# Five instruction lists written out as a table, in place of a planner, for a linear-attention and snake-MLP kernel

## The chip, the cores and the metric

The kernel runs on one core of one Trainium2 chip. The metric is the device time of one execution in microseconds; lower is better. The engines are PE (TensorE matmul, with PEld its weight loads), ACT (ScalarE), DVE (VectorE), POOL (GpSimd) and SP (SyncE, which here only issues DMAs).

## The reference

Two stages. First a blocked linear attention with decay over q, k, v of shape (4, 8, 768, 64):

```python
intra = np.einsum('bhic,bhjc->bhij', qb, kb) * Dmask[None]
intra = np.einsum('bhij,bhjd->bhid', intra, vb)
inter = np.einsum('bhid,bhde->bhie', qb * lam_pow[None], kv_state)
out[:, :, sl] = intra + inter
kv_state = lam_block * kv_state + np.einsum('bhsd,bhse->bhde', kb_dec, vb)
```

Its output, as x of 3072 tokens by 512, goes through an MLP with a snake activation, d_ff = 2048:

```python
h = x @ w_in
s = np.sin(alpha * h)
g = h + s * s / (alpha + 1e-09)
return g @ w_out
```

Inputs and output are float32; the kernel multiplies in bf16.

## The kernel before, in words

The attention works on 24 blocks of 128 tokens, six for each of 4 batches. For each block q and k are scaled by decay factors (`scale_block`, on POOL and DVE) and v is cast (ACT); q and k are transposed, on PE for the first blocks and by a DMA transpose on SP from block 12 on (`piece_T`, L565); then PE makes the masked scores, the block's output and the state (`piece_G`), DVE masks the scores (Sm, L687), and ACT or DVE copies the state (Zd, Zc) and the output (xT) out of PSUM. Loads are issued by SP (L379), those of the later weights by POOL.

The MLP works on 6 chunks of 512 tokens. `unit_A` and `unit_A2` make one tile of h: PE multiplies into a PSUM bank (L886, L920), ACT takes the sine (t16), ACT or POOL squares it (u16), and DVE adds h and writes gT (`scalar_tensor_tensor`, L903 and L938); that last step frees the bank. In the later chunks these products rotate over banks 4, 5 and 6. The second product is `unit_B` (L951) for chunks 0 and 1. For chunks 2 to 5 it is a scheme with seven products i of half size (`unit_P`, L1039) in place of eight, on sums of weights (`weight_sums`, L994) and sums of tokens (`token_sums`, L1017, on POOL or DVE); `finish` and `finish_half` (L1085, L1061, DVE) combine the products into osb rows and issue the stores (SP, some on ACT, L1089, L1094, L1063; stores of chunks 0 and 1 by ACT at L971).

All work is recorded first, as 1040 operations by `op(...)`, numbered from 0 in the order of the calls, each with what it reads and writes, so that dependences are known. Some operations name several engines that may run them. Then `_settle` decides the engine of each and the order on every engine, and `emit` writes the instructions in this order; where an operation depends on another engine, it waits on a semaphore. On every engine the instructions run in the order written. Before the change `_settle` is a planner on the host: it walks through modelled time, gives each engine its next ready operation by preference, and `MOVES` shifts the preferences of groups of operations. Dependences alone make the result right, so any order that keeps them computes the same.

Numbers used below: 99 cast of the second quarter of w1; 124, 130 the `unit_A2` of chunk 0 for its tokens 0 to 255 and 256 to 511; 136, 140, 163 `unit_A` of chunk 0; 138 a square and 139 an L903 step of chunk 0; 198, 200 casts of v, 215 and 218 a block's k transposed and copied, 221 a `piece_G`, 238 a copy to osb; 239, 240, 243, 244, 247, 248, 324, 325 stores of chunk 0; 290 a copy to xT; 204, 205, 339, 415, 422, 547 loads of k or v; 559, 595 to 597, 788 token sums; 594, 609, 613 L903 steps; 599 a `unit_B` of chunk 1; 604 a sum of weights; 635 a `unit_A` of chunk 3 into bank 4; 770 a cast of v. In the last chunk: 1031, 1034, 1037 the products i = 7 (the second token half in two parts), 1032, 1035, 1038 the subtractions after them and 1033, 1036, 1039 their stores; 1014, 1017, 1020 the stores of i = 5; 1027, 1030 those of the rows of i = 2 and 6.

Of the kernel before, what the change touches and what calls it, by code (L numbers as in the profile page):

```python
# [33 lines left out]
class _Plan:  # L34

    AHEAD = 40
    WINDOW = {"PE": 0.3, "ACT": 0.1, "DVE": 0.1, "POOL": 0.1}
    PIPE = {"ACT": 0.11, "DVE": 0.09, "POOL": 0.045, "PE": 0.0}
    HOP = {"PE": 0.055, "ACT": 0.035, "DVE": 0.035, "POOL": 0.075, "SP": 0.1}
    DRAIN = 0.085  # L40
    MOVES = (
        (633, 30, "any", 60), (169, 3, "all", 60), (138, 30, "all", -100), (112, 1, "SP", -10),
        (104, 1, "all", 210), (421, 3, "SP", -5), (967, 30, "PE", 145), (272, 3, "all", -155),
        (442, 3, "all", 60), (352, 30, "all", -145), (807, 3, "all", -15), (534, 10, "all", -15),
        (957, 30, "all", -25), (281, 30, "all", -55), (232, 30, "all", 40), (680, 1, "PE", 40),
        (1000, 3, "all", 55), (486, 1, "DVE", 55),
    )
    SPIN = ((0.095, 112, 5.0), (0.056, 128, 9.4), (0.216, 512, 1e9))
# [32 lines left out]
    @staticmethod  # L81
    def _transfers(order):

        queues = {}
        for o in order:
            if o.dma is not None:
                queues.setdefault(o.eng, []).append(o)
        left = {e: [[o.start + o.lag, o.runs, o.dur / o.runs, o] for o in sorted(q, key=lambda o: o.start)]
                for e, q in queues.items()}
        now, lands = 0.0, {}  # L90
        while any(left.values()):
            heads = [q[0] for q in left.values() if q]
            on = [h for h in heads if h[0] <= now]
            later = [h[0] for h in heads if h[0] > now]
            if not on:
                now = min(later)
                continue
            turn = sum(h[2] for h in on)
            step = min([h[1] * turn for h in on] + [t - now for t in later])
            now += step  # L100
            for h in on:
                h[1] -= step / turn
                if h[1] < 1e-6:
                    lands[h[3]] = now + h[3].lat
                    left[h[3].eng].pop(0)
        return lands

    def _settle(self):

        prio = {o: i - o.lead for i, o in enumerate(self.ops)}  # L110
        for at, width, kind, by in self.MOVES:
            for o in self.ops[at:at + width]:
                if (kind == "all" and o.given != "SP") or o.given == kind or (kind == "any" and not isinstance(o.given, str)):
                    prio[o] += by
        lands, best = {}, None
        for _ in range(10):
            order, new, off = self._pass(prio, lands)
            if best is None or off < best[0]:
                best = off, order, [(o, o.eng, o.start, o.done) for o in order]
            if off < 0.5:  # L120
                break
            lands = new
        for o, eng, start, done in best[2]:
            o.eng, o.start, o.done = eng, start, done
        return best[1]

    def _pass(self, prio, lands):
        for o in self.ops:
            o.eng, o.start, o.done = o.given, None, None
        order = self._order(prio, lands)  # L130
        new = self._transfers(order)
        return order, new, sum(abs(t - o.done) for o, t in new.items())

    def _order(self, prio, lands):
        num = {o: i for i, o in enumerate(self.ops)}
        waits = {o: len(o.deps) for o in self.ops}
        after = {}
        for o in self.ops:
            for d in o.deps:
                after.setdefault(d, []).append(o)  # L140
        clock = {e: 0.8 for e in ("PE", "SP", "ACT", "DVE", "POOL")}
        wire, port = 0.0, 0.0
        filler = self.filler
        sp = sorted((o for o in self.ops if o.eng == "SP"), key=lambda o: (prio[o], num[o]))
        pe = [o for o in self.ops if o.eng == "PE"]
        place = {o: i for i, o in enumerate(pe)}
        left = len(self.ops)
        can = {o for o in self.ops if not waits[o]}
        at = {}

        def ready(o, e):
            t = clock[e]
            for d in o.deps:
                if d.eng == e and (e == "PE" or d.dma is not None):
                    t = max(t, d.done)
                else:
                    t = max(t, d.done + self.HOP[e] + (self.DRAIN if d.eng == "PE" else 0.0))
            return t

        order = []  # L160
        nsp, npe = 0, 0
        while left:
            while npe < len(pe) and pe[npe].start is not None:
                npe += 1
            per = {e: [] for e in clock}
            for o in can:
                if o.eng == "SP":
                    if o is sp[nsp]:
                        per["SP"].append((at.setdefault(o, ready(o, "SP")), 0, o, o.dur))
                    continue  # L170
                if isinstance(o.eng, str):
                    e, d = o.eng, o.dur
                    if e == "PE" and place[o] >= npe + self.AHEAD:
                        continue
                    t = ready(o, e)
                else:
                    _, e, t, d = min((ready(o, e) + d + late, e, ready(o, e), d) for e, d, late in o.eng)
                if o.port:
                    t = max(t, port)
                per[e].append((t, prio[o], o, d))  # L180
            best = None
            for e, c in per.items():
                if not c:
                    continue
                soon = min(x[0] for x in c) + self.WINDOW.get(e, 0.0)
                x = min((x for x in c if x[0] <= soon), key=lambda x: (x[1], num[x[2]]))
                if best is None or x[0] < best[0]:
                    best = x[0], x[2], e, x[3]
            t, o, e, dur = best
            if e == "SP":  # L190
                t = max(t, clock["SP"])
                nsp += 1
            if e == "PE" and filler is not None:
                emit, reads, last = filler
                if last.start is not None:
                    filler = None
                else:
                    deps = [self.writer[b] for b in reads]
                    free = max([clock["PE"]] + [d.done + self.HOP["PE"] if d.done is not None else t for d in deps])
                    one, cols = next((d, n) for d, n, end in self.SPIN if free < end)  # L200
                    n = int((t - free) / one)
                    if n > 0:
                        f = _Op("PE", lambda h, n=n, cols=cols: emit(h, n, cols), one * n, tuple(reads), (), None, (), 0, 0)
                        f.deps = set(deps)
                        f.start, f.done = free, free + one * n
                        order.append(f)
            o.eng, o.start = e, t
            if o.dma is not None:
                clock[e] = t + o.issue
                wire = max(wire, t + o.lag) + o.dur  # L210
                o.done = max(t + o.lag + o.dur + o.lat, lands[o]) if o in lands else wire + o.lat
            else:
                o.done = t + dur
                clock[e] = o.done - self.PIPE[e]
                if o.port and e != "ACT":
                    port = o.done
            order.append(o)
            can.discard(o)
            left -= 1
            for s in after.get(o, ()):  # L220
                waits[s] -= 1
                if not waits[s]:
                    can.add(s)
        return order
# [48 lines left out]
def bass_lightning_attn__then__act_snake_kernel(  # L273
# [38 lines left out]
    with es:  # L312
# [15 lines left out]
        t16 = ring("t16", RU, [128, TCH], BF16)  # L328
        u16 = ring("u16", RU, [128, TCH], BF16)
# [8 lines left out]
        v32 = sb("v32", [128, RL * H * D], F32)  # L338
        qk2 = sb("qk2", [128, R2, 2 * H, D], BF16)
        v2 = sb("v2", [128, R2, H, D], BF16)  # L340
# [27 lines left out]
        def _(_unused_eng):  # L368
# [4 lines left out]
            op = P.op  # L373
# [84 lines left out]
            last = {}  # L458
# [22 lines left out]
            for i in range(3):  # L481
                t, ks = (4, 2) if i < 2 else (2, 1)
# [31 lines left out]
            def ported(o):  # L514
                o.port = True
                return o
# [793 lines left out]
```

## Time and profile before

| what | us |
|---|---|
| median of 3 runs (lowest to highest) | 213.34 (212.63 to 217.04) |
| profiled execution, its own time | 213.08 |
| its span in the profile | 211.3 |
| PE busy | 202.5 |
| ACT, DVE, POOL busy | 162.7, 151.2, 148.5 |
| mean granted PE clock | 0.999 |

Span is the time from the first to the last instruction of the program; the execution's own time has 1.8 us more around it. A row of a group gives the count after x, then busy time and mean duration in ns; a row of a wait gives who waited, for whom, the sum in us, how often, and the longest. In a table of stretches each engine's busy us is followed by its number of instructions, then the granted PE clock, the share of the DMA engines and GB/s. In a timeline a row has start, duration, engine, line, operation and tiles.

### The profile page before, as it was taken

To read this page: it belongs to the slowest core of one execution; us is meant where nothing else is said; L and a number is where in the kernel's file an instruction comes from. 1 tells how busy PE (TensorE), PEld (TensorE's weight loads), DVE (VectorE), ACT (ScalarE), POOL (GpSimd) and SP (SyncE) were. 2 spreads that over 40 slices of the span, in tenths; PEclk is the share of its full clock that TensorE was granted. 3 is DMA by queue.
4 is the path that set the end of the run, shared out by engine and by line. 5 is a ranking of instruction groups with operands and counts; after the bars stand their busy time and mean duration, and the time that the engine had idled before them with its cause. 6 is when DMAs were issued, how large, how long until landed. Compare 5 with 4: busy or idle time off the path is not lost.

```text
span 211.3 us, 4847 instructions
## 1 busy us (share of the span) xinstructions
PE 202.5 (96%) x1947; PEld 134.7 (64%) x1975; DVE 151.2 (72%) x237; ACT 162.7 (77%) x306; POOL 148.5 (70%) x147
## 2 busy tenths in 40 slices
PE   7988999999999999999999999999999999999995
PEld 7955534446677775645447677666667656666994
DVE  4884567684879896699989697565777657847553
ACT  4859895745988998798977998989698789767001
POOL 7085369583597668388998979879973678976660
PEclk9999999999999999999999999999999999999999
DMA  4999999999999999999969591335000050000514
GB/s 144 309 318 228 206 212 228 230 213 288 244 243 263 241 208 253 182 246 220 232 141 259 91 174 27 64 133 105 5 0 3 2 199 0 3 0 0 200 52 149
DMA packets 78998, 33.35 MB, mean 158 GB/s; under 512 B 55408, under 2 KB 76160, under 8 KB 78976
## 3 DMA queue, kind: packets, MB, share of 16 engines
q1 hardware_dynamic: 73744, 27.14, 56.6%
q0 software_dynamic: 3696, 3.67, 10.6%
q10 hardware_dynamic: 1536, 2.24, 3.3%
q8 instruction: 15, 0.25, 0.5%
q14 instruction: 7, 0.06, 0.1%
HBM read 27.28 MB, written 6.29 MB: 159 GB/s over the span
## 4 chain that ended last, share of the span: by engine, by line
PE 65%; ACT 13%; DVE 11%; DMA 3%; SPq 3%; issue 2%; ACTq 1%; POOL 0%
PE bank L1039 21%; PE bank L886 20%; PE bank L951 9%; PE bank L920 6%; DVE gT L903 5%; DMA v<-in_v_dram 3%; SPq L379 3%; PE bank L780 2%; PE bank L676 2%; ACT t L930 2%; ACT u L900 2%; ACT t L896 2%; ACT Zd L730 2%; DVE Xs L1017 1%; ACT v L559 1%
## 5 line engine op out<-in xcount | busy, mean ns | idle before, releaser
L903 DVE SCALAR_TENSOR_TENSOR gT<-u,rinv,bank 128x512 bf16<-128x512 bf16 x74 | 54.0, 743 | 26.7 <-ACT u L900 26.5
L886 PE MATMUL bank<-xT,w 128*128 128x512 bf16 x277 | 68.3, 379 | 2.3 <-DVE w L448 0.5
L896 ACT ACTIVATE t<-bank,alpha 128x512 bf16<-128x512 f32 x74 | 49.4, 683 | 14.0 <-PE bank L886 12.8
L1017 POOL TENSOR_TENSOR gT<-gT 128x512 bf16<-128x512 bf16 x37 | 43.1, 1175 | 8.1 <-DVE gT L903 3.7
L886 PEld LDWEIGHTS bank<-xT,w 128*128 128x128 bf16 x296 | 28.2, 98 | 29.5 <-DVE gT L903 2.3
L900 ACT ACTIVATE u<-t 128x512 bf16<-128x512 bf16 x66 | 41.0, 630 | 2.4 <-DVE gT L903 0.9
L1017 POOL TENSOR_TENSOR Xs<-gT 128x512 bf16<-128x512 bf16 x23 | 27.3, 1185 | 10.5 <-DVE gT L903 10.1
L687 DVE TENSOR_TENSOR Sm<-bank,mask 128x1024 bf16<-128x1024 f32 x24 | 29.0, 1220 | 4.0 <-PE bank L676 1.6
L951 PE MATMUL bank<-w,gT 128*128 128x512 bf16 x122 | 30.0, 379 | 0.3
L920 PE MATMUL bank<-xT,w 128*128 128x256 bf16 x176 | 22.6, 273 | 0.3 <-DVE gT L938 0.3
L536 POOL TENSOR_TENSOR qk<-q,Lq 128x512 bf16<-128x512 f32 x20 | 21.9, 1115 | 1.0 <-DMA q<-in_q_dram 1.0
L938 DVE SCALAR_TENSOR_TENSOR gT<-u,rinv,bank 128x256 bf16<-128x256 bf16 x44 | 18.8, 474 | 4.5 <-ACT u L934 2.5
L556 POOL TENSOR_TENSOR qk<-k,Lk 128x512 bf16<-128x512 f32 x20 | 21.2, 1068 | 0.0
L935 POOL TENSOR_TENSOR u<-t 128x512 bf16<-128x512 bf16 x8 | 8.3, 1040 | 18.3 <-ACT t L930 15.0
L930 ACT ACTIVATE t<-bank,alpha 128x256 bf16<-128x256 f32 x44 | 18.5, 475 | 2.7 <-PE bank L920 1.8
L951 PEld LDWEIGHTS bank<-w,gT 128*128 128x128 bf16 x128 | 12.0, 98 | 12.1
L920 PEld LDWEIGHTS bank<-xT,w 128*128 128x128 bf16 x176 | 15.9, 98 | 3.6 <-DVE gT L938 0.7
L1039 PE MATMUL bank<-ws,gT 128*128 128x256 bf16 x128 | 16.1, 273 | 0.0
L1039 PE MATMUL bank<-w,Xs 128*128 128x256 bf16 (+1 forms) x136 | 16.0, 267 | 0.0
L1039 PE MATMUL bank<-w,gT 128*128 128x256 bf16 (+1 forms) x136 | 16.0, 266 | 0.0
L1039 PEld LDWEIGHTS bank<-w,gT 128*128 128x128 bf16 x136 | 12.6, 98 | 3.3
L1039 PEld LDWEIGHTS bank<-ws,gT 128*128 128x128 bf16 x128 | 12.4, 98 | 3.0 <-DVE gT L903 0.2
(100 smaller groups left out, 268.4 us busy)
## 6 DMA issues: line engine op xcount, KB each, us to landing
q<-in_q_dram SPq DMA_DIRECT2D x12, 512.0 KB, 5.7
k<-in_k_dram SPq DMA_DIRECT2D x24, 256.0 KB, 5.8
v<-in_v_dram SPq DMA_DIRECT2D x24, 256.0 KB, 5.6
out_dram<-osb SPq DMA_DIRECT2D x14, 256.0 KB, 2.2
w<-in_moe_w_out_dram POOLq DMA_DIRECT2D x4, 512.0 KB, 11.4
w<-in_moe_w_in_dram POOLq DMA_DIRECT2D x3, 512.0 KB, 10.7
ws<-in_moe_w_in_dram SPq DMA_DIRECT2D x2, 512.0 KB, 7.5
out_dram<-osb ACTq DMA_DIRECT2D x8, 128.0 KB, 4.3
```

Source lines behind the costliest of these rows:

```text
L536: lambda e, a=a: e.tensor_tensor(qk2[:, j:j + 2, 4 * a:4 * a + 4, :], q32[:, jq, 4 * a:4 * a + 4, :, :].rearrange("p h t d -> p t h d"), b ...
L556: lambda e: e.tensor_tensor(qk2[:, j, H:2 * H, :], block32(k32, jl), lk, ALU.mult), 1.05,
L687: op("DVE", lambda e: e.tensor_tensor(Sm[js][:, :, :], banks[:, 512 * b0:512 * b0 + 1024].rearrange("p (c i) -> p c i", i=128), bass.AP(ma ...
L886: ins = e.matmul(ps[hb][:, c0:c1], w1[:, kc, 128 * m:128 * (m + 1)], xT[x][:, kc, c0:c1], start=(kc == 0 and c0 == lo), stop=(kc == NKC - ...
L896: op("ACT", lambda e: e.activation(t16[ju][:, w], ps[hb][:, w], ACTF.Sin, scale=alpha[:, m:m + 1]), 0.69 if hi - lo == TCH else 0.475, [ba ...
L900: lambda e: (e.activation(u16[ju][:, w], t16[ju][:, w], ACTF.Square) if e is nc.scalar else e.tensor_tensor(u16[ju][:, w], t16[ju][:, w], ...
L903: op("DVE", lambda e: e.scalar_tensor_tensor(out=gT[g][:, m, w], in0=u16[ju][:, w], scalar=rinv[:, m:m + 1], in1=ps[hb][:, w], op0=ALU.mul ...
L920: ins = e.matmul(ps[hb][:, 256 * i:256 * i + 256], w1[:, kc, 128 * (m + i):128 * (m + i + 1)], xT[x][:, kc, lo:lo + 256], start=(kc == 0 a ...
L930: op("ACT", lambda e, i=i: e.activation(t16[ju][:, 256 * i:256 * i + 256], ps[hb][:, 256 * i:256 * i + 256], ACTF.Sin, scale=alpha[:, m + ...
L951: ins = e.matmul(ps[ob][:, w], gT[g][:, m, 128 * s4:128 * (s4 + 1)], w2[:, m, w], start=(m == 0), stop=(m == NM - 1),)
L1017: e.tensor_tensor(dst, in0, in1, alu), 0, rd, wr))
L1039: ins = e.matmul(ps[ob][:, lo + d0:lo + d1], lhs, rhs[:, d0:d1], start=first and p == 0, stop=(p == NM // 2 - 1), skip_group_check=True)
```

## The change

The planner (`AHEAD` to `SPIN`, `_transfers`, `_pass`, `_order`) goes. `ORDER` holds for each engine a list of operation numbers; a pair in PE's list is a run of filler matmuls, and these are as many as before. The new `_settle` only walks through the five lists and takes from each as long as the dependences of the next operation are met:

```diff
+    def _settle(self):
+
+        left = {e: list(table) for e, table in self.ORDER.items()}
+        order, done = [], set()
...
+            for e, table in left.items():
+                while table:
...
+                        o = self.ops[table[0]]
+                        assert o.given == e or e in (x[0] for x in o.given)
+                    if not o.deps <= done:
+                        break
+                    table.pop(0)
+                    o.eng = e
+                    done.add(o)
+                    order.append(o)
```

The five lists have 249 operations on PE (as before), 305 on ACT (318 before), 265 on DVE (237), 128 on POOL (143) and 93 on SP (93). 80 operations have another engine than before. Parts of the lists:

```diff
+        "PE": (
...
+            (3,512), 65, 67, 69, 70, (3,512), 73, 75, 78, 80, 82, 85, (2,512), 87, 90, 91, 93, 124, 130, 136,
+            140, 144, 147, 151, 155, 159, 167, 175, 163, 230, 228, 171, 229, 232, 233, 231, 183, 187, 191, 179,
...
+            970, 966, 976, 972, 977, 985, 989, 990, 996, 994, 1002, 1004, 1006, 1010, 1012, 1018, 1008, 1015,
+            1021, 1028, 1025, 1023, 1034, 1031, 1037,
...
+        "ACT": (
...
+            176, 172, 173, 165, 184, 185, 188, 192, 189, 180, 145, 193, 181, 210, 218, 198, 238, 200, 224, 223,
+            225, 242, 246, 240, 274, 273, 214, 275, 254, 253, 265, 266, 267, 220, 248, 303, 302, 291, 290, 244,
+            247, 294, 293, 323, 295, 284, 283, 285, 328, 327, 324, 343, 315, 314, 263, 316, 309, 243, 308, 310,
+            239, 372, 281, 353, 354, 366, 355, 365, 367, 345, 346, 347, 394, 393, 387, 386, 402, 397, 375, 376,
...
+            943, 948, 949, 944, 954, 955, 963, 971, 964, 967, 968, 973, 974, 978, 997, 995, 1022, 1024, 1039,
+            1020,
...
+        "DVE": (
...
+            535, 554, 553, 552, 558, 509, 589, 566, 581, 602, 571, 604, 559, 594, 595, 597, 596, 609, 613, 618,
...
+            991, 980, 983, 982, 1005, 1003, 984, 1001, 1007, 998, 1013, 1000, 1011, 1009, 1016, 1026, 1029,
+            1019, 1035, 1032, 1038,
...
+        "SP": (
...
+            121, 203, 122, 120, 201, 202, 123, 338, 360, 337, 204, 421, 205, 361, 413, 414, 339, 420, 492, 456,
+            425, 454, 415, 546, 455, 496, 519, 461, 518, 422, 493, 520, 550, 525, 619, 620, 574, 665, 573, 695,
+            572, 667, 696, 623, 547, 579, 672, 666, 699, 737, 729, 738, 754, 755, 771, 884, 867, 866, 883, 988,
+            987, 992, 993, 1033, 1036, 1017, 1030, 1014, 1027,
```

Besides, three kinds of operations (casts of v, squares) get the mark `ported`, which the old planner read and nothing reads now.

More of the change, by code (lines that the diff above doesn't have):

```diff
@@ L34 @@
 class _Plan:
[L36 to L48, printed above, removed]
+    ORDER = {
[15 rows of a table added]
+        ),
+        "ACT": (
[16 rows of a table added]
+        ),
+        "DVE": (
[14 rows of a table added]
+        ),
+        "POOL": (
[7 rows of a table added]
+        ),
[6 rows of a table added]
+        ),
+    }
     def __init__(self, engines, new_sem):
@@ L79, in op @@
         return o
[L81 to L90, printed above, removed]
-        while any(left.values()):
[L92 to L223, printed above, removed]
@@ new lines, in _settle @@
+    def _settle(self):
+        left = {e: list(table) for e, table in self.ORDER.items()}
+        order, done = [], set()
+        emit, reads, _ = self.filler
+        assert sum(isinstance(i, int) for table in left.values() for i in table) == len(self.ops)
+        while any(left.values()):
+            before = len(order)
+            for e, table in left.items():
+                while table:
+                    if isinstance(table[0], tuple):
+                        n, cols = table[0]
+                        o = _Op("PE", lambda h, n=n, cols=cols: emit(h, n, cols), 0, tuple(reads), (), None, (), 0, 0)
+                        o.deps = {self.writer[b] for b in reads}
+                    else:
+                        o = self.ops[table[0]]
[6 more added lines that the diff above has]
+                    order.append(o)
+            assert len(order) > before
@@ L549, in scale_block @@
                     for a in range(2) if s % 2 == 0 else ():
-                        op("ACT" if s and not a else "POOL", lambda e, a=a: (e.copy if e is nc.scalar else e.tensor_copy)(
+                        ported(op("ACT" if s and not a else "POOL", lambda e, a=a: (e.copy if e is nc.scalar else e.tensor_copy)(
                             v2[:, j:j + 2, 4 * a:4 * a + 4, :],
                             pair32(v32, jl, a).rearrange("p h t d -> p t h d")), 0.62,
-                           [("v32", jl + a)], [("v2", j, a), ("v2", j + 1, a)])
+                           [("v32", jl + a)], [("v2", j, a), ("v2", j + 1, a)]))
                     return
@@ L557, in scale_block @@
                    [("k32", jl), "Lk"], [("k2", j, 0), ("k2", j, 1)]))
-                op((("ACT", 0.62, 0.0), ("POOL", 1.05, 0.3)) if s > 11 else "ACT",
+                ported(op((("ACT", 0.62, 0.0), ("POOL", 1.05, 0.3)) if s > 11 else "ACT",
                    lambda e: (e.copy if e is nc.scalar else e.tensor_copy)(v2[:, j, :, :], block32(v32, jl)), 0.62,
-                   [("v32", jl)], [("v2", j, 0), ("v2", j, 1)])
+                   [("v32", jl)], [("v2", j, 0), ("v2", j, 1)]))
             def piece_T(s, tb):
@@ L898, in unit_A @@
                    [bank(hb), "alpha"], [("t16", ju, 0), ("t16", ju, 1)])
-                op((("POOL", 1.04 * f, 0.0), ("ACT", 0.63 * f, 0.2)),
+                ported(op((("POOL", 1.04 * f, 0.0), ("ACT", 0.63 * f, 0.2)),
                    lambda e: (e.activation(u16[ju][:, w], t16[ju][:, w], ACTF.Square) if e is nc.scalar else
                               e.tensor_tensor(u16[ju][:, w], t16[ju][:, w], t16[ju][:, w], ALU.mult)), 0,
-                   [("t16", ju, 0), ("t16", ju, 1)], [("u16", ju)])
+                   [("t16", ju, 0), ("t16", ju, 1)], [("u16", ju)]))
                 op("DVE", lambda e: e.scalar_tensor_tensor(
@@ L932, in unit_A2 @@
                         scale=alpha[:, m + i:m + i + 1]), 0.475, [bank(hb), "alpha"], [("t16", ju, i)])
-                op((("POOL", 1.04, 0.0), ("ACT", 0.63, 0.3)),
+                ported(op((("POOL", 1.04, 0.0), ("ACT", 0.63, 0.3)),
                    lambda e: (e.activation(u16[ju][:, :], t16[ju][:, :], ACTF.Square) if e is nc.scalar else
                               e.tensor_tensor(u16[ju][:, :], t16[ju][:, :], t16[ju][:, :], ALU.mult)), 0,
-                   [("t16", ju, 0), ("t16", ju, 1)], [("u16", ju)])
+                   [("t16", ju, 0), ("t16", ju, 1)], [("u16", ju)]))
                 for i in range(2):
```

39 rows, old and new, of the table ORDER are left out of this document.

## The prediction

> **What bounds the kernel now.** I read the page first, then busy time by stretches, the waits of PE, and the timeline of the last microseconds. The page and the stretches:
>
> ```profile
> span 211.3 us, 4847 instructions
> PE 202.5 (96%) x1947; PEld 134.7 (64%) x1975; DVE 151.2 (72%) x237; ACT 162.7 (77%) x306; POOL 148.5 (70%) x147
> ```
>
> ```profile
> 20.00:30.00 10.00, 9.17 (x50) 4.58 (x53) 4.71 (x9) 9.25 (x19) 4.55 (x5) 1.00 1.23 208
> ...
> 40.00:50.00 10.00, 9.49 (x88) 5.10 (x89) 7.65 (x10) 5.54 (x11) 6.69 (x5) 1.00 1.03 248
> 50.00:60.00 10.00, 9.51 (x110) 6.53 (x111) 6.99 (x13) 7.74 (x18) 4.25 (x5) 1.00 1.04 261
> ```
>
> PE is the bound. The order cannot change how many matmuls there are, and the granted clock is 1.00 in every stretch, so only PE's gaps can shrink. Summed over the eighteen stretches from 20 to 200 us PE is idle for 180 - 176.51 = 3.5 us; the three stretches above hold 1.83 of it. The first 19 us are not in play: on every engine the table starts with the same instructions as the old list (the first differing one ran at 20.2 us on PE, 20.0 on ACT, 21.5 on DVE, 24.8 on POOL, 44.4 on SP). PE's waits after the start:
>
> ```profile
> PE bank L886 <- DVE w L448: 0.5, 1, 0.5
> PE bank L758 <- ACT v L559: 0.4, 1, 0.4
> PE bank L886 <- DVE gT L903: 0.3, 1, 0.3
> ...
> PE bank L920 <- DVE gT L938: 0.3, 1, 0.3
> ```
>
> Each is a single short wait, so there is no long one to take away. The end, by engine:
>
> ```profile
> 207.03 1.20 SPq L1094 DMA_DIRECT2D out_dram<-osb  x2
> 208.37 0.34 SPq L1089 DMA_DIRECT2D out_dram<-osb  x1
> 208.76 0.45 SPq L1063 DMA_DIRECT2D out_dram<-osb  x1
> 208.81 0.29 DVE L1061 TENSOR_TENSOR osb<-kept,bank 128x128 f32<-128x128 f32 x1 [0.16 <-PE bank L1039]
> 209.13 0.34 ACTq L1063 DMA_DIRECT2D out_dram<-osb  x1
> ```
>
> The page's DMA issues (KB of one, median us to landing):
>
> ```profile
> out_dram<-osb SPq DMA_DIRECT2D x14, 256.0 KB, 2.2
> out_dram<-osb ACTq DMA_DIRECT2D x2, 64.0 KB, 1.7
> ```
>
> PE ends at 208.79, the last 64 KB store is issued at 209.13, lands after about 1.7 us (210.8), and the span ends 0.5 us later at 211.3. The other stores of the last rows went out one by one before, the first of the last six at 202.29.
>
> **The change, part by part.** The sum is made against the profiled execution, 213.08 us (span 211.3 and 1.8 around it); the median of the runs is 213.34, 0.3 more.
>
> (1) **The last stores on SP: +2.3 us.** Old order of the last six: 1014, 1017, 1027, 1030, 1033, 1036, by readiness. The table has 1033, 1036, 1017, 1030, 1014, 1027. SP issues in order, so 1017, 1030, 1014 and 1027 now queue behind 1033, which waits for the subtraction 1032, which waits for product 1031, the last but one on PE. In the old order 1031 stood before half product 1034 (0.50 us); now it stands behind it, so 1032 ends at 208.34 + 0.50 = 208.84 instead of 208.34. Only then six issues follow at about 0.39 us each (208.37 to 208.76 above): the last, 1027 of 256 KB, at 208.87 + 5 x 0.39 = 210.8. With 2.2 us to land and 0.5 to close, the span ends at 213.5: +2.2. By volume: 896 KB from SP and 128 KB from ACT, 1.05 MB, at the 341 GB/s that the stretch 209 to 210 moved, take 3.1 us from about 209.7 (in the old tail bytes flowed some 0.85 us behind the issue); last byte 212.8, close 1.0 later, +2.4. I take 2.3; bounds 1.9 (each landing in 1.7) and 3.0 (issues 0.5 us apart, as the first loads on SP are). ACT's store 1020 moves behind 1039 for the same reason, but lands by 211.3 and hides under SP's. The Trainium skill, page "DMA: Bandwidth & Descriptors", section "Anatomy of one DMA", fits one DMA (issued from GpSimd) as 2.0 us plus bytes at 436 GB/s; by that estimate the last store takes 2.6 instead of the row's 2.2 and the tail costs 0.4 more.
>
> (2) **Start of the first products: -0.4 us.** Old PE order 124, 140, 144, 130; new 124, 130, 136, 140. Product 140 waited 0.5 us for the cast of the second quarter of w1 (first wait row; the cast ends at 20.16). Product 130 needs only the first cast and evictions that end at 19.82, when PE leaves 124. What is late next is bank 3 for product 163: its old gap at 28.4 us was 0.5. By the new ACT and DVE lists (square 138 on ACT, then 139) the bank is free near 28.5 with PE there near 28.2: -0.2.
>
> (3) **ACT's stores leave the stretch 45 to 57: -0.4 us.** The ACT timeline has
>
> ```profile
> 49.26 2.54 ACTq L971 DMA_DIRECT2D out_dram<-osb  x4
> 51.85 0.62 ACT L559 CAST v<-v 128x512 bf16<-128x512 f32 x1 [2.12 <-issue]
> ```
>
> four issues in a row, 0.6 us each, with 2.1 us in which ACT computes nothing. PE then loses 0.26 us to gT L938 at 54.8 and 0.18 (0.43 for the weights) to qkT L580 at 56. The table issues 240 and 248 alone, 244 and 247 behind eviction 290, and 239 and 243 some 16 to 21 us later, behind work that ran at 65. The next writes to those osb buffers ran at 79.9 us and later, so the delay is free; 325, which falls 42 us to about 103, still has 7 us before its buffer is written at 110.3. The gain is at most the 0.49 us that PE idles in 50 to 60; I take 0.4.
>
> (4) **Work changes engine.** 80 instructions do. Of the token sums 27 go from POOL to DVE and 6 back: POOL loses 21 x 1.18 = 24.8 us, DVE gains 21 x 0.79 = 16.7 (20 sums took 15.9 us there). Squares: 15 from ACT to POOL, 11 back; 11 copies out of PSUM go from ACT to DVE, 3 back; two qkT copies go to ACT, one away. Outside one stretch this lies beside PE's work: in 172 to 200 DVE goes from 18.3 to about 26 of 28 us while POOL falls by 11. The exception:
>
> ```profile
> 90.00:120.00 30.00, 29.57 (x244) 16.51 (x248) 27.39 (x38) 26.90 (x51) 27.52 (x25) 1.00 1.01 208
> ```
>
> The sums on DVE (shortest, median, longest ns):
>
> ```profile
> L1017 DVE TENSOR_TENSOR gT<-gT x11: 495/787/1158, 94.5 to 203.8; 128x512 bf16<-128x512 bf16 x11
> L1017 DVE TENSOR_TENSOR Xs<-gT x9: 410/760/1255, 92.9 to 197.3; 128x512 bf16<-128x512 bf16 x9
> ```
>
> DVE has 27.4 of 30 us already. The moves add net 2 sums (1.6), 3 evictions of xT (2.2) and one of Zd (0.4): 31.6 of 30. Inside it, weight sum 604 now stands ahead of 559, 594, 595, 597, 596, 609 and 613, and it cannot start before product 599 leaves PE at 109.6. Behind it 0.7 + 1.0 + 0.7 + three sums of 0.5 to 0.9 + two steps L903 of 0.74 put the end of 613 between 115.2 and 116.4, and product 635 needs its bank 4 at 115.2. **New wait of PE: +1.0 us** (near the upper end, since sums of this stretch took 0.95 on average), bounds 0 (the sums run at 0.41 and DVE catches up) and 4.2 (the whole 1.6 and the 2.6 us that DVE idles today). The Trainium skill, "SBUF — State Buffer", section "SBUF: two separate sides", calls the port pair of VectorE and GpSimd an exclusive lock: one full instruction blocks the other. By it the spread 410 to 1255 is waiting for POOL, and 21 fewer sums on POOL would shorten those on DVE; the two sums at 0.41 are 0.8 us less and the stretch still holds 30.8.
>
> (5) **Loads and transposes on SP and POOL: 0.** SP is busy issuing without a pause from 25 to 81 us, so a load's place fixes when it lands. Setting the old landing times against the new places by cumulated bytes, the worst margins to a first reader are those of 204, 205 and 339, at -0.2, -0.2 and -0.6 us; the scalings and casts behind them feed PE 6 us later or more. 415, 422 and 547 fall 9 to 18 us behind transposes, but their casts feed PE at 99.5, 104.9 and 135. POOL's two w2 loads move by one or two places. Bounds 0 and 1.
>
> (6) The planner's code itself runs on the host, and the added port marks have no reader left: 0.
>
> Sum: 213.08 + 2.3 - 0.4 - 0.2 - 0.4 + 1.0 = **215.4 us**, 1.0% above the median; its own range is 213.8 to 216.8.
>
> **The rivals.**
> A. DVE becomes the bound in 90 to 120: part 4 at 4.2 instead of 1.0, 218.6. For it: 31.6 of 30 us, sums of that stretch at 0.95 on average. Against it: banks 4, 5 and 6 rotate over about 5.5 us while a product's steps need 3.5, so 2 us of lateness cost nothing.
> B. The other side: the table closes PE's gaps. All 3.5 us from 20 to 200 and the 0.4 before vanish: 213.08 + 2.3 - 3.9 = 211.5, not slower than before. It decides from 2.3 us of closed gaps on. For it: the gaps are single waits of 0.2 to 0.5, each fit for one moved instruction. Against it: parts 2 and 3 name 1.0 only, and the other waits sit on chains that the table leaves alone, such as 215, 218, 198, 238, 200 ahead of 221 at 45 us.
> C. The lists leave no slack anywhere: PE idles all along as in 20 to 60 (1.83 in 40 us), 8.7 in 190 us instead of 3.5: 220.6. For it: sum 788 stands 28 us and cast 770 30 us later than it ran. Against it: each still ends ahead of its reader in the old times.
> D. The change does not do at the end what the table says, and the six stores leave early: 215.4 - 2.3 = 213.1. In-order issue speaks against it.
>
> **How the numbers follow.** Forecast 0.57, A 0.17, B 0.15, C 0.07, D 0.04. A measurement of this kernel tells about 2% from no change: 209.1 and 217.6 around the median. Over 217.6 lie two thirds of A and nearly all of C, 0.17; under 209.1 only a B with more gain than the gaps hold, 0.02; within, 0.81. The range 211.8 to 218.2 leaves out a third of B, half of A and C: 0.2.
>
> **What would show it.** Right: SP issues its last six stores in one run from about 208.9 less what PE gained, DVE's last subtraction lies over 3.5 us ahead of the span's end (2.2 today), no four L971 issues in a row, no wait for w L448, and a wait of PE on gT L903 near 115. Wrong: PE's idle time in 20 to 200 under 2 us (B), or over 6 (C); DVE without idle time in 90 to 120 and PE below 28 of 30 there (A); the stores L1089 and L1063 of i = 5 issued on SP before 206 (D).

## The result, and the profile after

The changed kernel takes 214.08 us (median of 7 runs, 213.93 to 215.14), the kernel before 212.80 us beside it on the same chip. The ratio is 1.0062, with a 95% interval of 1.0034 to 1.0090: 0.6% slower, too little to tell from no change at 2%, and a loss all the same. A few executions ran at a lower granted clock (222.11 us at 0.969 in experiment 12) and are left out of the ratios. The forecast was 215.4, 1.1% above 213.08. The profiled execution took 214.13 us (213.08 before). In the new listing every line number of the kernel's body is 64 smaller (L886 is L822, L1039 is L975, L1017 is L953).

The page, span and busy times:

```profile
span 212.4 us, 4846 instructions
...
PE 202.3 (95%) x1948; PEld 134.5 (63%) x1975; DVE 160.7 (76%) x265; ACT 156.8 (74%) x293; POOL 128.6 (61%) x132
```

The stretches (length, then busy us of PE, PEld, DVE, ACT and POOL with their instructions, granted clock, DMA share and GB/s):

```profile
20.00:30.00 10.00, 9.94 (x55) 4.93 (x56) 5.35 (x10) 8.83 (x17) 5.91 (x6) 1.00 1.23 207
40.00:50.00 10.00, 9.89 (x94) 5.47 (x94) 8.66 (x11) 6.75 (x14) 5.14 (x5) 1.00 1.02 240
50.00:60.00 10.00, 9.95 (x132) 7.44 (x131) 7.81 (x15) 8.31 (x19) 5.72 (x6) 1.00 1.04 257
90.00:120.00 30.00, 29.58 (x251) 17.05 (x253) 26.51 (x40) 26.59 (x48) 21.48 (x19) 1.00 1.09 223
```

PE's gaps closed in all three of the early stretches (9.17, 9.49 and 9.51 before). From 20 to 200 us PE now idles 1.9 us instead of 3.5. In 90 to 120 DVE has *less* to do than before (26.5 of 30 us, 27.4 before), not the 31.6 of the prediction. Waits of PE that are left after the first one, at 1.5 us:

```profile
PE bank L648 <- ACT Zd L666: 0.9, 1, 0.9
PE bank L822 <- issue: 0.5, 3, 0.2
...
PE bank L822 <- DVE gT L839: 0.2, 1, 0.2
```

The waits for w and for v are gone, and no new one stands near 115. The wait for Zd, near 16 us, lies ahead of the first instruction that differs; kernels with the same order up to there show it with 0.34 to 0.91 us, so it is no effect of the change. The end, by engine (start, length):

```profile
207.28 0.29 DVE L997 TENSOR_TENSOR osb<-kept,bank 128x128 f32<-128x128 f32 x1
207.29 0.33 SPq L1025 DMA_DIRECT2D out_dram<-osb  x1
...
207.66 0.93 SPq L999 DMA_DIRECT2D out_dram<-osb  x2
208.63 0.45 SPq L1030 DMA_DIRECT2D out_dram<-osb  x1
209.12 0.45 SPq L1025 DMA_DIRECT2D out_dram<-osb  x1
209.61 0.45 SPq L1030 DMA_DIRECT2D out_dram<-osb  x1
```

PE ends at 207.25 us, 1.5 earlier than before (208.77). DVE's last subtraction ends at 207.57, and then SP still issues stores for 2.5 us whose data had in part been ready for long: the first of the old order, 1014, had its data at 200.7 and goes out at 209.12. From PE's end to the end of the span it takes 5.14 us instead of 2.57. So -1.5 and +2.6 make the +1.1 of the two spans.

### The profile page after: what moved, and what is told of

It reads as the page before. It is cut to its first block, busy times and chain, and to the rows that moved or that the text cites. A ratio compares the mean times of both kernels' runs of the same rounds, so it can differ in the third digit from the quotient of the medians.

```text
span 212.4 us, 4846 instructions
## 1 busy us (share of the span) xinstructions
PE 202.3 (95%) x1948; PEld 134.5 (63%) x1975; DVE 160.7 (76%) x265; ACT 156.8 (74%) x293; POOL 128.6 (61%) x132
## 4 chain that ended last, share of the span: by engine, by line
PE 83%; ACT 4%; DMA 3%; SPq 3%; DVE 3%; issue 2%
PE bank L822 28%; PE bank L975 20%; PE bank L887 13%; PE bank L856 9%; DMA v<-in_v_dram 3%; PE bank L716 3%; SPq L315 3%; PE bank L612 3%; PE bank L694 1%; PE bank L511 1%; ACT t L832 1%; DVE gT L839 1%; ACT u L836 1%; PE bank L534 1%; PE bank L656 1%
## 5 line engine op out<-in xcount | busy, mean ns | idle before, releaser
L822 PE MATMUL bank<-xT,w 128*128 128x512 bf16 x281 | 68.2, 379 | 1.3 <-issue 0.5
L839 DVE SCALAR_TENSOR_TENSOR gT<-u,rinv,bank 128x512 bf16<-128x512 bf16 x74 | 53.3, 743 | 20.7 <-ACT u L836 16.1
L832 ACT ACTIVATE t<-bank,alpha 128x512 bf16<-128x512 f32 x74 | 49.3, 683 | 19.5 <-PE bank L822 19.0
L822 PEld LDWEIGHTS bank<-xT,w 128*128 128x128 bf16 x296 | 27.9, 98 | 29.4 <-DVE gT L839 2.0
L836 ACT ACTIVATE u<-t 128x512 bf16<-128x512 bf16 x61 | 37.4, 627 | 1.2
L623 DVE TENSOR_TENSOR Sm<-bank,mask 128x1024 bf16<-128x1024 f32 x24 | 28.9, 1216 | 0.8 <-PE bank L612 0.5
L953 POOL TENSOR_TENSOR gT<-gT 128x512 bf16<-128x512 bf16 x20 | 24.1, 1222 | 8.7 <-DVE Xs L953 7.7
L837 POOL TENSOR_TENSOR u<-t 128x512 bf16<-128x512 bf16 x13 | 13.5, 1039 | 25.4 <-ACT t L832 25.4
L953 POOL TENSOR_TENSOR Xs<-gT 128x512 bf16<-128x512 bf16 x19 | 22.3, 1184 | 6.7 <-DVE gT L839 6.2
L874 DVE SCALAR_TENSOR_TENSOR gT<-u,rinv,bank 128x256 bf16<-128x256 bf16 x44 | 18.8, 475 | 6.7 <-ACT u L870 5.6
L887 PEld LDWEIGHTS bank<-w,gT 128*128 128x128 bf16 x128 | 11.9, 98 | 12.0
L871 POOL TENSOR_TENSOR u<-t 128x512 bf16<-128x512 bf16 x7 | 7.3, 1038 | 14.6 <-ACT t L866 9.5
L975 PE MATMUL bank<-ws,gT 128*128 128x256 bf16 x128 | 15.9, 273 | 0.0
L975 PE MATMUL bank<-w,Xs 128*128 128x256 bf16 (+1 forms) x136 | 15.8, 266 | 0.0
L953 DVE TENSOR_TENSOR gT<-gT 128x512 bf16<-128x512 bf16 x28 | 15.7, 574 | 0.1
L975 PE MATMUL bank<-w,gT 128*128 128x256 bf16 (+1 forms) x136 | 15.5, 266 | 0.0
```

Source lines behind the costliest of these rows:

```text
L623: op("DVE", lambda e: e.tensor_tensor(Sm[js][:, :, :], banks[:, 512 * b0:512 * b0 + 1024].rearrange("p (c i) -> p c i", i=128), bass.AP(ma ...
L822: ins = e.matmul(ps[hb][:, c0:c1], w1[:, kc, 128 * m:128 * (m + 1)], xT[x][:, kc, c0:c1], start=(kc == 0 and c0 == lo), stop=(kc == NKC - ...
L832: op("ACT", lambda e: e.activation(t16[ju][:, w], ps[hb][:, w], ACTF.Sin, scale=alpha[:, m:m + 1]), 0.69 if hi - lo == TCH else 0.475, [ba ...
L836: lambda e: (e.activation(u16[ju][:, w], t16[ju][:, w], ACTF.Square) if e is nc.scalar else e.tensor_tensor(u16[ju][:, w], t16[ju][:, w], ...
L839: op("DVE", lambda e: e.scalar_tensor_tensor(out=gT[g][:, m, w], in0=u16[ju][:, w], scalar=rinv[:, m:m + 1], in1=ps[hb][:, w], op0=ALU.mul ...
L874: op("DVE", lambda e, i=i: e.scalar_tensor_tensor(out=gT[g][:, m + i, lo:lo + 256], in0=u16[ju][:, 256 * i:256 * i + 256], scalar=rinv[:, ...
```

## The experiments

Each kernel is either the new table with an edit, or the old order, written out as a table, with an edit; in the listings of the second sort a line number is 66 smaller than in the kernel before. Each ratio is to the kernel before, run beside it. All the differences are small: no ratio is clear of 2%, and two intervals (experiments 3 and 6) reach across it. PE's end, the spans and all lines are of one profiled execution. The new kernel did not run again beside these; "over the new kernel" is against its 214.08.

**1. The last stores in order of readiness, in the new table.**

```diff
 "SP":  ..., 992, 993,
-    1033, 1036, 1017, 1030, 1014, 1027,
+    1014, 1017, 1027, 1030, 1036, 1033,
 "ACT": ..., 1022, 1024,
-    1039, 1020,
+    1020, 1039,
```

> The new table with only the last stores back in order of readiness: on SP 1014, 1017, 1027, 1030, 1036, 1033, and on ACT 1020 ahead of 1039. Theory (the queue behind 1033 costs the tail 2.6 us): the last issue is ACT's 1039 at 207.6, and as in the kernel before the span ends 2.2 us after that issue, at 209.8; 209.8 + 1.7 around it = 211.5, some 0.6% under the kernel before. Rival (the last rows' bytes set the end, whatever their order): SP and ACT still have about 1 MB to move after PE's end and the time stays within 0.5 of 214.1.

Measured: 211.81 us, ratio 0.9932 (0.9907 to 0.9956). Its timeline at the end:

```profile
core 0 of [0], span 210.0 us
...
205.12 1.54 SPq L1030 DMA_DIRECT2D out_dram<-osb  x2
...
206.53 1.36 ACTq L999 DMA_DIRECT2D out_dram<-osb  x2
206.72 0.41 SPq L999 DMA_DIRECT2D out_dram<-osb  x1
...
207.25 0.38 SPq L1025 DMA_DIRECT2D out_dram<-osb  x1
```

SP is done at 207.63 instead of 210.06, and the span falls by 2.4 us at the same end of PE (207.21). This is the theory's number; the bytes do not set the end. Of all kernels here it is the fastest against the old one (0.7% below it; experiment 11 is 0.3% below): the order in the middle is a gain, the order of six stores throws it away.

**2. Only the new order of the last stores in the old kernel.** SP's last six become 1033, 1036, 1017, 1030, 1014, 1027, and ACT's 1020 goes behind 1039.

> The old order on every engine (written out as a table), with only the last six SP stores in the new order 1033, 1036, 1017, 1030, 1014, 1027 and ACT's 1020 behind 1039. Theory: six issues from 208.37 on, 0.48 us apart as in the new kernel, so the last at 210.8, the end 2.2 to 2.6 behind it at 213.2: 2.0 to 2.4 us slower than the kernel before, about 215.1. Rival (the new kernel's loss sits in its middle, by the work that changed engines): within 0.5 of 213.

Measured: 215.86 us, ratio 1.0125 (1.0091 to 1.0159). PE ends at 208.73, SP issues from 208.32 to 211.08 with 0.46 us from one issue to the next on average, and the span is 213.5, 2.2 longer than before. This is the theory's result again, from the other side.

**3. The token sums back on their old engines, in the new table.** 27 sums leave DVE for POOL and 6 go the other way; the first of these moves:

```diff
 "DVE":  ..., 469,
+    473,
     498, 517, 506,
-    472,
     491, ..., 594,
-    595,
     597, ..., 638,
-    557,
     603, ...
 "POOL": ..., 460,
-    473, 471, 507, ..., 508, 510, 598,
+    471, 472, 507, ..., 508, 595, 598, ...
```

> The new table with the token sums back on their old engines (27 from DVE to POOL, 6 from POOL to DVE), each put into the other list at the time at which it ran. Theory (a DVE sum is long only while POOL runs): POOL is busy some 25 us more, the sums left on DVE lengthen from a mean of 0.59 towards 0.79 us, and the time rises by 0.5 to 2 us because squares on POOL queue behind sums. Rival (the length of a DVE sum has nothing to do with POOL): the sums left keep a mean near 0.59; by the prediction's arithmetic the time then falls, as DVE is relieved.

Measured: 217.03 us, ratio 1.0187 (1.0149 to 1.0225). The sums on DVE by form (shortest, median, longest ns), first in the new kernel, then here:

```profile
L953 DVE TENSOR_TENSOR gT<-gT x28: 407/419/1374, 94.5 to 200.6; 128x512 bf16<-128x512 bf16 x28
L953 DVE TENSOR_TENSOR Xs<-gT x13: 407/425/1380, 102.2 to 196.4; 128x512 bf16<-128x512 bf16 x13
```

```profile
L953 DVE TENSOR_TENSOR gT<-gT x11: 407/605/1358, 95.1 to 201.3; 128x512 bf16<-128x512 bf16 x11
L953 DVE TENSOR_TENSOR Xs<-gT x9: 413/632/1425, 91.2 to 197.5; 128x512 bf16<-128x512 bf16 x9
```

The shortest stays where it was, the medians rise by half, and the mean goes from 0.59 to 0.75 us ((8.0 + 7.1)/20), as the theory said. In the new kernel the 21 sums during which POOL does nothing take 407 to 425 ns, all of them; the 20 that meet an instruction of POOL take 417 to 1380. PE ends 2.9 us later. It waits 1.5 us for POOL's sums, for which it does not wait in the new kernel, and in 180 to 200 POOL is busy 19.5 of 20 us; it also waits 1.0 us more for DVE (gT L839 and kept L992), the rest is not traced to a wait. The rival, by which DVE is relieved and the time falls, is out.

**4. POOL kept busy from 106.4 to 112 in the new table.**

```diff
 "POOL": ..., 508, 510,
+    1040, 1041, 1042, 1043,
     598, ...
...
+scr = maskf[:, :, :].rearrange("p a b -> p (a b)")[:, 0:TCH // 2].bitcast(BF16)
+for late in (581, 581, 581, 581):
+    op("POOL", lambda e: e.tensor_tensor(scr, w1[:, 0, 0:TCH], w1[:, 1, 0:TCH], ALU.add), 1.16, ...,
+       after=(P.ops[late],))
```

> The new table with four additional sums of 128x512 on POOL, written to a tile that nobody reads any more, placed so that POOL is busy from about 106.4 to 111, where DVE runs weight sum 604 and token sums 559, 595, 597 and 596 at 0.42 us each. Theory (shared access of DVE and POOL): these four lengthen to 0.8 to 1.2 and weight sums 602 and 604 to 1.2 or more, 613 ends about 2 us later, and PE waits 1 to 2 us for gT L839 ahead of product 635, which is the wait that the prediction had put there; 0.5 to 2 us in the total. Rival (the sums were long before for a reason of their own, such as their place in DVE's queue): they stay at 0.42 and the total moves by under 0.3.

Measured: 215.57 us, ratio 1.0107 (1.0078 to 1.0137), 1.5 us over the new kernel. Its timeline, lines of POOL, DVE and PE:

```profile
106.47 5.69 POOL L1217 TENSOR_TENSOR maskf<-w 128x512 bf16<-128x512 bf16 x4 [1.29 <-DVE Sm L623]
...
108.48 1.38 DVE L953 TENSOR_TENSOR gT<-gT 128x512 bf16<-128x512 bf16 x1
...
110.43 2.00 DVE L953 TENSOR_TENSOR Xs<-gT 128x512 bf16<-128x512 bf16 x2
...
113.49 0.40 PE L694 MATMUL bank<-qkT,Zd 128*128 128x128 bf16 x4 [1.01 <-DVE gT L839]
```

The same stretch of the new kernel:

```profile
108.35 0.42 DVE L953 TENSOR_TENSOR gT<-gT 128x512 bf16<-128x512 bf16 x1
...
109.34 0.75 DVE L953 TENSOR_TENSOR Xs<-gT 128x512 bf16<-128x512 bf16 x2
...
110.17 1.27 POOL L953 TENSOR_TENSOR gT<-gT 128x512 bf16<-128x512 bf16 x1 [4.99 <-DVE Xs L953]
```

Three sums that take 0.42 + 0.75 us there (two in one line) take 1.38 + 2.00 here, and PE waits 1.0 us for DVE's gT: the predicted wait, at the predicted size, one product earlier than named (the block 624, which starts 0.05 or 0.06 us behind the end of 609 in both kernels, ahead of 635). It is there only when POOL works beside these sums. Some of the expected lengths missed: 602 had begun 0.16 us ahead of POOL and stayed at 0.67, 604 went to 0.84 only, and the fourth sum, 596, began when POOL was done and stayed at 0.41.

**5. The same with 604 late.** In that kernel 604 goes behind 618 on DVE.

> The kernel with four additional sums on POOL from 106.4 to 112, in which PE waited 1.0 us for gT L839 near 113, now with weight sum 604 on DVE behind 618 as in the old list instead of ahead of 559, 594, 595, 597, 596, 609 and 613. Theory (the wait is the sum of long DVE sums and 604 ahead of them): without 604 the chain is 0.7 to 0.85 us shorter, 613 ends so much earlier, the wait falls to 0.2 to 0.4 and the total by 0.6 to 0.8 against that kernel, to about 214.8. Rival (the wait comes from the long sums alone, or from POOL's own later work): the wait stays at 0.8 to 1.0 and the total near 215.6.

Measured: 215.48 us, ratio 1.0125 (1.0093 to 1.0156), against 215.57 without the move. The wait ahead of the block is 0.98 us, so this is the rival's result. The four sums start sooner and fall wholly beside POOL's work: 0.71 + 1.71 + 1.37 us, the same 3.79 in all as 1.38 + 2.00 + 0.41. DVE's step 609 starts 0.5 us earlier, which only takes away a wait of 0.3 ahead of product 615. The place of 604, on which the prediction had built its new wait, hardly matters.

**6. Two weight sums as before, in the new table.** 432 back on POOL ahead of 211, and 431 on DVE ahead of mask product 216.

```diff
 "DVE":  ..., 430,
+    431,
-    216, 433, 432, 222, 227, 431,
+    216, 433, 222, 227,
 "POOL": ..., 197,
+    432,
     211, ...
```

> The new table with two weight sums as before: 432 on POOL ahead of 211 instead of on DVE, and 431 on DVE ahead of mask product 216 instead of behind 432. Theory (the 0.4 us at 45 us was a wait for 216, late because 431 on DVE took 1.9 us instead of 0.7 beside 432 on POOL, and not for cast 198): 431 takes 1.2 to 2 us, 216 ends 1.2 to 2 us later than in the new kernel, at 45.5 to 46.3, and PE waits 0.8 to 1.5 us ahead of 221: +0.5 to +1.5 in the total. Rival (the wait was for the cast on ACT, as the line of the profile says): 198 is where it is in the new kernel, no wait, no change.

Measured: 216.93 us, 1.0187 with a wide interval (1.0121 to 1.0252). The profiled execution is the fastest of the four, 215.21; in it PE's end is 1.08 us later than in the new kernel, and what the others lose beyond that (up to 218.44) is not traced. The timeline, lines of POOL, DVE and PE:

```profile
41.27 2.12 POOL L930 TENSOR_TENSOR ws<-w 128x1024 bf16<-128x1024 bf16 x1 [1.69 <-DMA w<-in_moe_w_out_dram]
42.30 1.64 DVE L930 TENSOR_TENSOR Ta<-w 128x1024 bf16<-128x1024 bf16 x1
...
44.46 1.21 DVE L623 TENSOR_TENSOR Sm<-bank,mask 128x1024 bf16<-128x1024 f32 x1
...
45.73 0.40 PE L694 MATMUL bank<-qkT,Zd 128*128 128x128 bf16 x4 [0.96 <-DVE Sm L623]
```

Here 430, a sum of the same form, is the one that meets POOL's 432 and takes 1.64 us; 431 behind it takes 0.68. 216 ends at 45.67 instead of 44.28, and PE waits for it, not for cast 198, which ends at 44.18. So the theory holds as to what waits for what, with the other sum as the late one.

**7. One weight sum moved in the old kernel.** 432 leaves POOL and stands behind 216 on DVE.

> The old order on every engine with one instruction moved: weight sum 432 from POOL to DVE, right behind mask product 216. Theory (216 was late because DVE's sum 431 took 1.9 us beside 432 on POOL): 431 takes 0.7 us, 216 ends at about 44.6 instead of 45.7, PE's wait of 0.41 us at 45 us goes, and PE ends 0.4 us earlier: some 0.2% off the kernel before, to be read in PE's busy time of 40 to 50 (9.9 instead of 9.5) rather than in the total. Rival (431 is long for a reason of its own): it keeps 1.9 us and nothing changes.

The kernel before at this place, lines of DVE, ACT (casts 198 and 200) and PE:

```profile
42.64 1.93 DVE L994 TENSOR_TENSOR ws<-w 128x1024 bf16<-128x1024 bf16 x1
44.49 1.21 DVE L687 TENSOR_TENSOR Sm<-bank,mask 128x1024 bf16<-128x1024 f32 x1
...
44.23 0.62 ACT L559 CAST v<-v 128x512 bf16<-128x512 f32 x1
...
45.23 0.63 ACT L559 CAST v<-v 128x512 bf16<-128x512 f32 x1
...
45.85 0.38 PE L758 MATMUL bank<-qkT,Zd 128*128 128x128 bf16 x4 [0.41 <-ACT v L559]
```

Measured: 212.60 us, ratio 0.9981 (0.9950 to 1.0011), 0.3 below the 212.92 beside it, which cannot be told from nothing. 431 takes 0.68 us instead of 1.93, 216 ends at 44.74, and the wait of 0.41 us is gone: PE starts 221 at 45.36. The casts are no earlier than before: 198 ends at 44.94 and 200 at 45.94, behind the start of 221. So neither of them was what PE waited for. PE's busy time of 40 to 50 rises to 9.66 only: behind 216, 432 and the next sum take 1.42 and 1.52 us, beside scalings on POOL. The profiled execution, at 213.76, also has a wait of 1.2 us for gT L872 at 65, whose cause is open.

**8 and 9. The start: PE's first products alone.** In the new table 124, 130, 136, 140, 144 becomes 124, 140, 144, 130, 136; in the old kernel the new order is put in. The first is not quite the old order, in which 136 stands three places further back, behind 155.

> The new table with the first products in PE's old order, 124, 140, 144, 130, 136 instead of 124, 130, 136, 140, 144; nothing else. Theory (the new order covers the cast of the second quarter of w1): the wait of PE for w L384 at 20 us comes back with 0.4 to 0.5 us, PE's idle time in 20 to 30 rises from 0.06 to about 0.5, and the total by 0.4 at most, since no other gap is there to take it up: 214.5. Rival (the gain at the start comes from ACT's and DVE's new order of evictions): no wait, under 0.2 us in PE's busy time of 20 to 30.

Measured: 215.57 us, ratio 1.0125 (1.0099 to 1.0150), 1.5 us over the new kernel's median. The wait for w comes back with 0.5 us, and a second of 0.7 us at 26, for gT L874, comes with it.

> The old order on every engine, with only PE's first products in the new order 124, 130, 136, 140, 144. The prediction's second term by itself: the wait of 0.47 us for w L448 at 20 us goes, -0.4. Rival (PE's order helps only together with the evictions that ACT and DVE do in step with it, as undoing it alone cost more than it can have brought): a new wait for a bank, by an eviction in the old order, takes its place; PE's busy time of 20 to 30 stays at 9.2 or falls.

Measured: 214.24 us, ratio 1.0068 (1.0040 to 1.0095): slower, by 1.3 us. From its timeline of PE:

```profile
21.04 1.67 PE L820 MATMUL bank<-xT,w 128*128 128x512 bf16 x7
...
28.20 1.90 PE L820 MATMUL bank<-xT,w 128*128 128x512 bf16 x8 [1.37 <-DVE gT L872]
```

The wait at 20 us is gone and 1.37 us are lost at 28, for a bank that ACT and DVE empty in the old order. The stretch 20 to 30, first of experiment 8, then of experiment 9:

```profile
20.00:30.00 10.00, 8.78 (x49) 4.22 (x50) 4.71 (x9) 7.44 (x15) 5.40 (x6) 1.00 1.23 207
```

```profile
20.00:30.00 10.00, 8.58 (x47) 4.05 (x48) 4.27 (x9) 7.99 (x16) 3.23 (x4) 1.00 1.23 208
```

PE is busy 9.17 us of this stretch with both orders old and 9.94 with both new, but 8.78 and 8.58 with one of each. PE's order and the order of the evictions are one edit: either half alone is worse than neither.

**10 and 11. ACT's six stores alone.** In the new table 239 and 240 go back behind cast 200 and 243, 244, 247, 248 behind 246; in the old kernel the six are spread as the table has them.

> The new table with ACT's six stores 239, 240, 243, 244, 247 and 248 where they were: 239 and 240 behind cast 200, the other four in a row behind 246. Theory (the prediction's third term): ACT computes nothing for 2 us near 48 to 50, PE waits 0.2 to 0.5 us in 50 to 60, +0.4 in the total at most. Rival (the gaps of 50 to 60 closed because the squares went to POOL and the copies to DVE): PE's busy time in 50 to 60 stays at 9.95 of 10.

Measured: 215.25 us, ratio 1.0114 (1.0085 to 1.0144), 1.2 us over the new kernel. ACT's timeline:

```profile
48.91 3.31 ACTq L907 DMA_DIRECT2D out_dram<-osb  x4
52.27 0.84 ACT L866 ACTIVATE t<-bank,alpha 128x256 bf16<-128x256 f32 x2 [2.90 <-PE bank L534]
```

Around the four issues (0.83 us each, 0.64 in the kernel before) ACT computes nothing for 2.9 us. In the new kernel it pauses 1.7 us ahead of the same step, for PE, so about 1.2 are the stores'. PE waits 0.6 us for Zd at 48.4 and 1.0 us for gT L874 at 55.1. The mechanism is the theory's, the size three times as large.

> The old order on every engine, with only ACT's six stores spread as in the new table: 240 behind 246, 248 behind 220, 244 and 247 behind 290, 243 behind 309, 239 behind 310. The prediction's third term by itself: ACT has no stretch of 2 us without work near 50, PE's busy time of 50 to 60 rises from 9.51 to 9.8 to 9.95, -0.4 in the total at most. Rival: the squares and copies that changed engine closed that gap, and PE's busy time there stays at 9.5.

Measured: 212.20 us, ratio 0.9968 (0.9946 to 0.9989), 0.7 below the 212.92 beside it. PE's busy time of 50 to 60 rises from 9.51 to 9.83, as expected. In 40 to 50 it rises as well (9.49 to 9.89), which is not the stores' doing: POOL's sum 432 started at 41.31 instead of 41.90, when its weights had landed, and 431 on DVE was through at 43.98, all ahead of the first store that moved. So of the 0.96 us by which PE ends earlier in this execution, 0.32 in 50 to 60 are the stores'.

**12. All three in the old kernel.**

> The old order with all three of these: 432 on DVE, PE's first products in the new order, ACT's six stores spread. If they are independent gaps, PE ends 1.0 to 1.3 us earlier than in the kernel before, at 207.5 to 207.8, and the time is 0.5 to 0.6% lower, as good as the new kernel with its stores put back. If they depend on the squares, copies and sums that changed engine, the gain is 0.5 us or less.

Measured: 213.82 us, ratio 1.0034 (1.0006 to 1.0063). PE ends at 209.60, later than before (208.77), so both outcomes that were expected missed: it is no gain at all. PE is busy 9.75 and 9.73 us in 40 to 50 and 50 to 60 (9.49 and 9.51 before), but 8.57 and 9.55 in 20 to 30 and 30 to 40 (9.17 and 10.00 before): PE's first products, without their evictions, cost more than the stores and the weight sum gain.

## Why the prediction was right, and where its steps were not

The forecast of 215.4, made against 213.08, missed the profiled 214.13 by 1.3 us. The direction and the main cause were right, but the forecast move of +2.3 was twice the measured +1.05. PE's end was forecast unchanged (-0.4 - 0.2 - 0.4 + 1.0) and came 1.5 us earlier; the tail came 0.3 us longer. With 0 in place of the +1.0 of term 4, and with the -0.4 of the wait that it left alone, the same sum gives 214.0.

- **Term 1, the last stores, +2.3: shown.** 2.2 us in the old kernel, 2.4 in the new one (experiments 1 and 2). The issues are 0.46 us apart on average, not 0.39. The other 0.2 of the +2.6 stay when the stores are put back: 2.8 us from PE's end to the end of the span, 2.6 before. The last store landed 2.2 us behind its issue (209.61 to 211.83). The Trainium skill, "DMA: Bandwidth & Descriptors", section "Anatomy of one DMA", gives an estimate of 2.6 for it, by a fit for DMAs issued from GpSimd; for this store from SP the measured 2.2 counts.
- **Term 2, the start, -0.6: right in size, wrong in its seat.** 20 to 30 us gained 0.77. But the -0.4 was put down to PE's order alone, and PE's order alone loses 1.3 us (experiment 9); that the size came out is in part luck.
- **Term 3, ACT's stores, -0.4: shown.** The stretch 50 to 60 gained 0.44, and 0.32 with the stores alone. Put back in the new table, the stores cost more, 1.2 us (experiment 10).
- **Term 4, DVE overfull in 90 to 120, +1.0: the failed step.** It priced every sum that went to DVE at 0.79 us and those of this stretch at 0.95, from rows of a kernel in which POOL was busy 27.5 of 30 us there, while the edit takes 21 sums off POOL. The prediction had named the lock on which this rests, but applied it to the two sums that the stretch gains and not to the eight that it already held. In the new kernel POOL idles from 105.2 to 110.2 and the sums beside 604 take 0.42 us each: 613 ends at 112.48, and product 635 starts at 113.2 without waiting for it. The nine sums on DVE in 90 to 120 take 4.9 us in all, where the prediction's sum had 7.7 for eight and 1.6 for two more; over the whole kernel 41 sums take 23.7 us and the 20 before took 15.9, so 21 more cost 7.8 us and not 16.7. Experiment 4 brings the wait by giving POOL its work back. The 27.4 of 30 us "busy" overstated the load: a sum's recorded time holds what it waits for POOL. All 20 sums of the kernel before took 15.9 us, and 20 x 0.42 = 8.4 would have done.
- **A wait held to be left alone, -0.4.** The prediction followed the line "PE bank L758 <- ACT v L559" to the chain on ACT with casts 198 and 200. Cast 198 had ended at 44.85, and PE went on at 45.85. What ended then was mask product 216 on DVE (44.49 to 45.70), late because 431 ahead of it took 1.93 us beside POOL. Cast 200 ended then as well, at 45.86, so the end times in one trace leave two candidates; experiment 7, in which 221 starts ahead of the end of 200, decides between them.
- **The rivals.** The prediction's own sign of being wrong for B (PE idle under 2 us in 20 to 200) was met, narrowly, with 1.9: 1.6 of the 3.5 us closed. So for the middle of the kernel B was nearer than the forecast. B's price of the tail was the forecast's, so it stopped 0.7 us of closed gaps short of "not slower". For A and C the traces show nothing, and six issues in one run refute D. The signs of being right held, but for the wait near 115.

## What the runs showed of the hardware

A bf16 sum of two 128x512 SBUF tiles on DVE takes 407 to 425 ns with POOL idle and up to 1425 beside it (experiment 3). Which of the two begins first decides. In the new kernel 20 sums overlap an instruction of POOL: the 6 that began ahead of it took 417 to 425 ns, and the 14 that began while it ran ended 0.28 or 0.29 us behind its end, every one. Forms that read a PSUM bank do not move: L839 takes 731 to 750 ns and L623 1202 to 1225 in the new kernel, whatever POOL does. A blocked sum of the larger form, 128x1024, also ends a fixed time behind POOL's instruction: POOL's 432 ended at 44.02, 43.43 and 43.39 (the kernel before, experiments 11 and 6), the weight sum on DVE that met it at 44.57, 43.98 and 43.94, each 0.55 us later, 0.13 less than the 0.68 that such a sum needs alone. POOL pays too: of the four sums of experiment 4 the two that began inside a weight sum of DVE took 1.53 and 1.49 us, the two that began in the last 0.2 us of a token sum 1.22, against a median of 1.16 for POOL's token sums of this size. That is the exclusive lock of the Trainium skill, "SBUF — State Buffer", section "SBUF: two separate sides", and the trace agrees with it: the one that comes second waits for the whole instruction.

## What to carry to other kernels

The last stores on an in-order DMA queue are best issued in the order in which their data are ready: one late store at the head of six cost more here (2.2 to 2.4 us) than all gaps closed in the middle gained (1.5). A DVE sum is priced by what POOL does at that moment in the *new* schedule, and a busy share that holds waits for another engine overstates the load. Before a wait is put down to the releaser that the profile names, its end time is held against the time at which the waiting engine went on, and where two end together, one of them is moved.
